# Segment attention written as four streams instead of a join after every unit

## The chip, the cores and the metric

The kernel runs on one core of a Trainium2 chip. The time is the device time of one execution in microseconds (us); the kernel before has a median of 3170.16 us over three runs (3165.81 to 3174.22). PE is TensorE, ACT is ScalarE, DVE is VectorE, POOL is GpSimd, and SP is SyncE, which here only issues DMAs.

## What is computed

Four layers follow each other, each with a layer norm ahead of it and a residual: A, B, A, B. Layer A is attention over the whole prompt with 32 query heads of width 16 that share one key and value head. Layer B cuts the 2048 rows into four segments of 512; each of its 32 heads attends within its segment (causal by segment) and also reads a memory that holds the key and value sums of the earlier segments.

```python
# A: prompt attention
scores = jnp.einsum("bhqd,bkd->bhqk", q, k) * (Dh ** -0.5)
o = jnp.einsum("bhqk,bkd->bhqd", softmax(scores), v)
...
# B: for each segment s
logits = jnp.einsum("bhqd,bhkd->bhqk", qs, ks) * scale + mask
a_dot = jnp.einsum("bhqk,bhkd->bhqd", softmax(logits), vs)
a_mem = einsum("bhld,bhde->bhle", phi(qs), M) / (einsum("bhld,bhd->bhl", phi(qs), z)[..., None] + 1e-6)
o = g * a_mem + (1.0 - g) * a_dot
M = M + jnp.einsum("bhld,bhle->bhde", phi(ks), vs)
z = z + phi(ks) summed over the segment
```

## The kernel before, in words

The host code writes the program as Python generators. Each generator yields a function that says from when PE may take its next piece, and the planner keeps rough clocks for PE, ACT, DVE and POOL (`clk`, `pe()`, `on()`) to choose which generator goes on. The order in which pieces are taken is nearly the order of the program on each engine; a scheduler behind it may still move single instructions forward or back.

Layer A works in units of four heads by 512 queries. For each of 16 key tiles of 128 keys a unit has scores on PE (L99/L102, operands qa and kst), two exps of 128 by 1024 on ACT (L752, into one of nine buffers named pa), and the product with the values (pa and va). These 1024 key tiles in all are the backbone. Beside them runs, for one segment at a time, `side`: the output projection of layer A and the norm, `b_block` (layer B's segment attention), the output projection of layer B, and the preparation of the next layer A. `weave` mixes the two in a given proportion. The last segment's `side` has no layer A work left beside it, so it runs alone at the end of the kernel.

`b_block` has eight units: pair t = n // 2 holds eight heads, and p = n % 2 picks four of them. These are the parts that the change touches, with the lines of the profile:

- inputs (`b_inputs`, one per pair): query and key projection (L455), their split into two fp16 parts (L551, L553), the way through DRAM (L893), the memory features ph (L907 to L909).
- row maxima (`rowmax`, from `b_load`, L933): the unit's scores once more on PE, a reduction per tile on DVE (L992; in the last block the masked form, L963, twelve reductions a unit, m), then the guard: a transposition on PE (L688), four small steps on DVE (L691 to L694), the maxima to DRAM (L696, mf) and back into two rows of the keys' and queries' tile (L698, qkb). `gr[n]` is the planner's time for that.
- scores (first half of `b_attend`): PE on qkb with 50 rows, so that the maximum is subtracted by the matmul, masks by idb and maskv, then six exps on ACT per unit (L1031). They take their space from the same nine pa buffers and the same two score banks as layer A (four banks, in two pairs).
- values and finish (second half of `b_attend`): PE on pa and vb, the transposition out of the bank on DVE (L1042), for all segments but the first the memory product (phq, ms; transposition L1051), the reciprocals and products (L1055 to L1067; in the last block L1062 to L1067 on POOL), and after a pair's second unit L1069, which puts the pair into otb. Then `b_memory` for odd units.

What sets the order of these is one line of `b_block`, a join per unit:

```python
for n in range(8):
    yield from par(rowmax(n + 2), unit(n), inputs(n // 2 + 2) if n % 2 == 1 and n // 2 + 2 not in hold else None)
```

`par` runs its generators together and ends when all have ended. So the scores and values of unit n, the maxima of unit n + 2, and for odd n the inputs of a later pair start together, and unit n + 1 starts when the last of them is through. Among the generators that are ready, `par` takes one whose matmuls have the form (the tiling of the PE array: rows, cols or full) that PE is in, else the first that is ready, else the one that is ready soonest. Ahead of the eight units stand the inputs of pairs 0 and 1 (in the last block of pair 2 too), the maxima of units 0 and 1, and the rest of the values' projection.

Of the kernel before, what the change touches and what calls it, by code (L numbers as in the profile page):

```python
# [89 lines left out]
def net_kernel(ctx, tc, x_in, a_wq, a_wk, a_wv, a_wo, b_wq, b_wk, b_wv, b_wo, b_beta, cst, out):  # L90
# [73 lines left out]
    LOAD = 2600.0  # L164
    LAG = 0.03
    DRAIN = 130.0
    FIRST = 3500.0
    PVL = 0.0
    PEND = 0.0
# [2 lines left out]
    tiling = ["full"]  # L172
# [211 lines left out]
    def form_of(need):  # L384
        return need.form() if isinstance(need, Need) else "full"

    def par(*gens):


        live = []  # L390
        for g in gens:
            if g is not None:
                try:
                    live.append([g, next(g)])
                except StopIteration:
                    pass

        def pick():
            ready = [z for z in live if z[1]() <= clk["pe"]]
            same = [z for z in ready if form_of(z[1]) == tiling[0]]  # L400
            return (same or ready or [min(live, key=lambda z: z[1]())])[0]

        while live:
            yield Need(lambda: min(z[1]() for z in live), lambda: form_of(pick()[1]))
            z = pick()
            try:
                z[1] = next(z[0])
            except StopIteration:
                live = [y for y in live if y is not z]
# [590 lines left out]

    b_ob = {}

    def b_attend(b, n, r, last):
        t, p = divmod(n, 2)
        exact = r["exact"]
        q, k = (qx, kx) if exact else (qb[n % 3], kb[n % 3])
        parts, held, tl = [], [], 0.0
        for kt in range(4):
            nq = 512 - kt * P
            es, loc = [], ([(0, 0), (1, 0)] if kt < 2 else [(0, 0), (0, nq)])  # L1010
            for s_ in range(1 if kt >= 2 else 2):
                yield Need(lambda: max(gr[n], rings["sc"].ready(), exps.ready()), "cols" if exact else "rows")
                ring = rings["sc"]
                z, sc = ring.take()
                for u in range(2):
                    if loc[u][0] != s_:
                        continue
                    o_ = loc[u][1]
                    if exact:
                        for i in range(2):  # L1020
                            by_triangle(i == 0, sc[:, i, o_:o_ + nq], k[0:98, 2 * u + i, kt * P:(kt + 1) * P],
                                        q[0:98, 2 * u + i, kt * P:512])
                        e_ = pe(2 * cols(nq) + 30, "cols")
                    else:
                        by_pairs(sc[:, :, o_:o_ + nq], k[:, u, kt * P:(kt + 1) * P], q[:, u, kt * P:512], 50, (0, 1),
                                 (maskv, 0))
                        e_ = pe(cols(nq) + 60, "rows")
                w = loc[1][1] + nq
                e = tmp(EXPS, [P, 2, 512], F32, "pa")
                held.append(exps.take()[0])  # L1030
                A.activation(e[:, :, 0:w], sc[:, :, 0:w], AF.Exp, scale=0.25 if exact else 0.25 / (UPB * UPB))  # L1031
                es.append(e)
                ring.free[z] = on("act", e_ + PEND, 51 + 1.667 * w)
                tl = ring.free[z] + HOP
            parts.append((kt, nq, es, loc))
        pvb, rel = yield from slot(None, max(tl, v_r[0]), "cols")
        for part in parts:
            b_pv(t, p, pvb, *part)
# [61 lines left out]
    def b_block(b, last, exact, norms):  # L1100

        hold = {}
        mem_done[:] = [-1] * 4

        def inputs(t):
            if t < 4:
                hold[t] = yield from b_inputs(b, t, exact, norms)

        def rowmax(*units):
            for n in units:  # L1110
                if n < 8:
                    need = b_load(hold[n // 2], n)
                    yield from b_rowmax(n, need, True) if exact else (b_rowmax_masked if last else b_rowmax)(n, need)

        def begin():
            yield from inputs(0)
            yield from rowmax(0, 1)

        def beside():
            yield from b_values((2, 3))  # L1120
            yield lambda: 0.0 if 0 in hold else 1e18
            yield from inputs(1)
            if last:
                yield from inputs(2)

        def unit(n):
            t = n // 2
            yield from b_attend(b, n, hold[t], last)
            if n % 2 == 1:
                yield from b_memory(b, t, hold[t])  # L1130

        if exact:
            yield from b_values((2, 3))
            for n in range(8):
                if n % 2 == 0:
                    yield from inputs(n // 2)
                yield from rowmax(n)
                yield from unit(n)
            return
        yield from par(begin(), beside())  # L1140
        if last:
            layout("b")
        for n in range(8):
            yield from par(rowmax(n + 2), unit(n), inputs(n // 2 + 2) if n % 2 == 1 and n // 2 + 2 not in hold else None)


    def everything(exact):
# [135 lines left out]
```

## Time and profile before

| | us |
|---|---|
| median of three runs | 3170.16 |
| the profiled execution | 3165.43 |
| its span, first to last instruction | 3163.6 |
| PE busy | 2796.1 |
| ACT busy | 2328.7 |
| DVE busy | 1554.7 |
| POOL busy | 269.4 |
| mean granted clock of PE | 0.976 |

The page shows one execution. Busy time is the union of an engine's instructions; a busy PE is not PE at its peak. The 40 slices of the page are 79 us each; a digit is the busy share or the granted clock in tenths. In a group's line the columns are line, engine, operation, output and inputs, count, busy time and mean ns, and the idle time of the engine ahead of the group with what ended it. In the chain each piece is start, duration, and what the end of the kernel waited for. Layer A's exps (L752) run from about 48 to about 2966 us; what comes after is the last segment's `side` alone. The exps of the eight blocks (L1031) begin at 481, 854, 1236, 1617, 2053, 2365, 2729 and 3036 us.

### The profile page before, as it was taken

Reading aid. Unit: us, or ns where it says so; the run is one execution under the profiler, and the core shown is the slowest. Engines: PE = TensorE matmul, PEld = TensorE weight load, DVE = VectorE, ACT = ScalarE, POOL = GpSimd, SP = SyncE. Lnnn points to the kernel's source line nnn. Section 1 sums busy time; section 2 is a strip of 40 time slices with the busy share of each in tenths; the row PEclk is TensorE's granted clock in tenths of the full one; section 3 lists DMA queues with packets and bytes.
Section 4 is the critical chain, followed back from the end, with each engine's and each line's share of the span. In section 5 each row is a group of like instructions: output and inputs, shape, how many; then the busy total and the mean of one; then the engine's idle time right before and its main releaser. Section 6 shows DMA issues by size and latency. Waiting matters only on the chain.

```text
span 3163.6 us, 115692 instructions
## 1 busy us (share of the span) xinstructions
PE 2796.1 (88%) x51714; PEld 1324.4 (42%) x51714; DVE 1554.7 (49%) x4463; ACT 2328.7 (74%) x2583; POOL 269.4 (9%) x437
## 2 busy tenths in 40 slices
PE   6988888899898998889998898888998899988987
PEld 3533344435443454334443344443443434433543
DVE  7621345534555435654365445464345533644455
ACT  4689778886778867887788878677687877878423
POOL 2100120001000010001100010000000000000111
PEclk9999999999999999999999999999999999999968
DMA  5320231113320233102331142320331114110331
GB/s 158 105 66 23 74 119 47 42 60 107 101 60 21 67 106 103 54 16 91 127 92 53 35 143 86 115 76 22 113 100 39 42 37 139 55 53 23 130 100 37
DMA packets 152444, 240.20 MB, mean 76 GB/s; under 512 B 26144, under 2 KB 101760, under 8 KB 151936
## 3 DMA queue, kind: packets, MB, share of 16 engines
q1 hardware_dynamic: 123520, 129.93, 13.6%
q0 software_dynamic: 28416, 102.77, 10.0%
q8 instruction: 407, 6.67, 0.9%
q14 instruction: 101, 0.83, 0.1%
HBM read 162.12 MB, written 70.52 MB: 74 GB/s over the span
## 4 chain that ended last, share of the span: by engine, by line
PE 38%; ACT 29%; issue 18%; DVE 8%; DMA 4%; POOL 1%; SPq 1%; DVEq 0%; ACTq 0%; POOLq 0%
ACT pa L752 25%; PE bank L99 17%; PE bank L455 13%; PE bank L102 7%; DVE mo L992 4%; ACT pa L1031 3%; DMA sb<-parts 2%; DVE m L963 1%; DMA xt<-in_A_x_dram 1%; DVE parts L553 1%; PE bank L515 0%; POOL parts L551 0%; DMA wst<-in_B_wq_dram 0%; DMA w<-wd 0%; PE bank L688 0%
## 5 line engine op out<-in xcount | busy, mean ns | idle before, releaser
L752 ACT ACTIVATE pa<-bank 128x1024 f32<-128x1024 f32 x2048 | 1947.2, 1107 | 469.6 <-PE bank L102 464.9
L102 PE MATMUL bank<-pa,va 64*17 64x512 f32 x14336 | 1101.7, 599 | 0.2 <-DVE t L791 0.2
L99 PE MATMUL bank<-pa,va 64*17 64x512 f32 x2048 | 1060.0, 598 | 10.3 <-ACT pa L752 5.8
L99 PE MATMUL bank<-qa,kst 49*32 49x512 f16 x2048 | 742.1, 382 | 179.0 <-ACT pa L752 146.9
L102 PE MATMUL bank<-qa,kst 49*32 49x512 f16 x14336 | 823.6, 387 | 0.8 <-DVE qmx L600 0.8
L992 DVE CUSTOM_DVE_ANT_0 mo<-bank,maskq 128x256 bf16<-128x256 f32 (+3 forms) x896 | 439.0, 490 | 223.3 <-PE bank L102 159.6
L99 PE MATMUL bank<-qkb 48*32 48x512 f16 (+7 forms) x1536 | 345.6, 311 | 111.1 <-DVE m L992 46.2
L102 PEld LDWEIGHTS <-kst 49*32 49x32 f16 x14336 | 227.6, 90 | 500.6 <-issue 489.5
L1031 ACT ACTIVATE pa<-bank 128x1024 f32<-128x1024 f32 (+2 forms) x384 | 323.3, 885 | 136.0 <-PE bank L102 133.1
L102 PE MATMUL bank<-qkb 50*32 50x512 f16 (+7 forms) x6656 | 367.8, 313 | 0.2 <-DMA qkb<-mf 0.2
L99 PEld LDWEIGHTS <-kst 49*32 49x32 f16 x2048 | 173.1, 92 | 371.2 <-issue 343.7
L455 PE MATMUL bank<-xh,w 128*128 128x512 f32 x832 | 285.6, 407 | 9.6 <-DVE w L319 4.8
L102 PEld LDWEIGHTS bank<-pa,va 64*17 64x17 f32 x14336 | 256.7, 94 | 24.7 <-DVE t L791 8.1
L455 PE MATMUL bank<-w,xh 128*128 128x512 f32 x752 | 247.5, 409 | 5.6 <-issue 4.1
L102 PEld LDWEIGHTS <-qkb 48*32 48x32 f16 (+1 forms) x6656 | 152.1, 94 | 222.8 <-issue 212.4
L99 PEld LDWEIGHTS bank<-pa,va 64*17 64x17 f32 x2048 | 185.5, 94 | 105.1 <-issue 15.5
L790 DVE STREAM_TRANSPOSE ts<-bank 128x512 f32<-128x512 f32 x88 | 62.9, 715 | 287.2 <-PE bank L102 286.9
L276 POOL DMA_DIRECT2D w<-wd x154 | 85.5, 556 | 1235.9 <-PE bank L455 1173.3
L455 PEld LDWEIGHTS bank<-xh,w 128*128 128x128 f32 x832 | 157.2, 189 | 79.8 <-issue 28.9
L99 PEld LDWEIGHTS <-qkb 48*32 48x32 f16 (+1 forms) x1536 | 129.2, 95 | 145.9 <-issue 109.6
L1042 DVE STREAM_TRANSPOSE t<-bank 128x512 f32<-128x512 f32 x64 | 45.9, 717 | 278.1 <-PE bank L102 278.1
L102 PE MATMUL bank<-pa,vb 128*17 128x384 f32 (+3 forms) x1920 | 173.5, 443 | 8.4 <-ACT pa L1031 7.6
(164 smaller groups left out, 2773.8 us busy)
## 6 DMA issues: line engine op xcount, KB each, us to landing
w<-wd POOLq DMA_DIRECT2D x154, 512.0 KB, 4.9
sb<-parts SPq DMA_DIRECT2D x192, 128.0 KB
qkb<-sb SPq DMA_DIRECT2D x256, 96.0 KB
wd<-w POOLq DMA_DIRECT2D x24, 512.0 KB, 3.9
x<-xt SPq DMA_DIRECT2D x48, 256.0 KB
xt<-x SPq DMA_DIRECT2D x48, 256.0 KB
qa<-sd SPq DMA_DIRECT2D x176, 66.0 KB
xt<-in_A_x_dram SPq DMA_DIRECT2D x32, 256.0 KB
```

What stands on the lines that cost most here:

```text
L99: nc.tensor.matmul(*a, **k)
L102: tc.keep_in_program_order(nc.tensor.matmul(*a, **k))
L276: G.dma_start(f(w), parts_d[kind, i])
L455: T.matmul(ps, lhsT=l_(kt), rhs=r_(kt), start=n == 0, stop=n == 11)
L553: V.scalar_tensor_tensor(parts[:, 1, :], x, up, parts[:, 0, :], op0=ALU.mult, op1=ALU.subtract)
L752: A.activation(x, sc, AF.Exp, scale=scale)
L790: V.transpose(ts.rearrange("p a b -> p (a b)"), pva[:, 0, :])
L963: V.reduce_max(m[:, u0:u0 + per, i, qt], ps[:, 0:per * nk].rearrange("p (h k) -> p h k", k=nk), axis=AX.X)
L992: V.tensor_tensor_reduce(out=mo[:, 0:nk], in0=ps[:, o_:o_ + nk], in1=maskq[:, 512 - nk:512], op0=ALU.add, op1=ALU.max, scale=1.0, scalar=- ...
L1031: A.activation(e[:, :, 0:w], sc[:, :, 0:w], AF.Exp, scale=0.25 if exact else 0.25 / (UPB * UPB))
L1042: V.transpose(t1.rearrange("p a b -> p (a b)"), pvb)
```

## The change

`b_attend` is cut in two: `b_scores` puts what it made into `scored[n]`, and `b_attend` takes it from there. The loop with its join goes. In its place `par` runs four generators from the first unit to the last, each with a condition of its own:

- `scores`: unit n when its maxima are written (`gr`) and n is at most one ahead of the finished units (AHEAD_S)
- `values`: unit n (values, finish, and the memory of odd units) when its scores are written
- `maxima`: unit n when the scores of unit n - 3 are written, n is at most two ahead of the finished units (AHEAD_M), and its inputs are there
- `pairs`: the inputs of pairs 2 and 3, when units 0 and 2 are finished

`par` gets an argument: with `same=False`, which the last block uses, it no longer prefers the form that PE is in, and takes the first ready generator in the order scores, values, maxima, pairs.

```diff
-    def par(*gens):
+    def par(*gens, same=True):
...
-            same = [z for z in ready if form_of(z[1]) == tiling[0]]
-            return (same or ready or [min(live, key=lambda z: z[1]())])[0]
+            alike = [z for z in ready if same and form_of(z[1]) == tiling[0]]
+            return (alike or ready or [min(live, key=lambda z: z[1]())])[0]
...
-    def b_attend(b, n, r, last):
-        t, p = divmod(n, 2)
+    def b_scores(n, r):
...
+        scored[n] = parts, held, tl
+
+    scored = {}
+
+    def b_attend(b, n, r, last):
+        t, p = divmod(n, 2)
+        parts, held, tl = scored.pop(n)
         pvb, rel = yield from slot(None, max(tl, v_r[0]), "cols")
...
-        for n in range(8):
-            yield from par(rowmax(n + 2), unit(n), inputs(n // 2 + 2) if n % 2 == 1 and n // 2 + 2 not in hold else None)
+        done = [0, 0]
+
+        def maxima():
+            for n in range(2, 8):
+                yield lambda: 0.0 if n <= done[0] + 2 and n <= done[1] + AHEAD_M and n // 2 in hold else 1e18
+                yield from rowmax(n)
+
+        def scores():
+            for n in range(8):
+                yield lambda: 0.0 if n in gr and n <= done[1] + AHEAD_S else 1e18
+                yield from b_scores(n, hold[n // 2])
+                done[0] = n + 1
+
+        def values():
+            for n in range(8):
+                yield lambda: 0.0 if n in scored else 1e18
+                yield from unit(n)
+                done[1] = n + 1
+
+        def pairs():
+            for t in range(2, 4):
+                yield lambda: 0.0 if done[1] >= 2 * t - 3 else 1e18
+                if t not in hold:
+                    yield from inputs(t)
+
+        yield from par(scores(), values(), maxima(), pairs(), same=not last)
```

The changed kernel has the same instructions on every engine, in another order; lines behind b_attend's second half are 8 higher, those between `par` and it 1 or 2 higher. Three places show what moves.

On DVE, in the last block, the end of unit 2's row maxima (m_52703, twelve reductions in all) and unit 0's finish (t_5248_53010). Before:

```order
L963 TENSOR_REDUCE m_52703<-bank 128x1
L692 SCALAR_TENSOR_TENSOR mrr_52690<-bank,mrr_52690 16x128
L693 TENSOR_REDUCE mmx_117<-bank 16x1
L694 TENSOR_TENSOR mmx_117<-mmx_117 16x1
L963 TENSOR_REDUCE m_52703<-bank 128x1 x5
L963 TENSOR_REDUCE m_52703<-bank 128x2 x4
L1042 STREAM_TRANSPOSE t_5248_53010<-bank 128x512
L691 TENSOR_SCALAR mrr_52985<-bank 16x128
```

After (unit 0's finish is t_5246_52905 to rr_52907; unit 1's begins with t_5260_53190):

```order
L965 TENSOR_REDUCE m_52703<-bank 128x1 x2
L1050 STREAM_TRANSPOSE t_5246_52905<-bank 128x512
L1053 COPY rr_52907<-t_5246_52905 128x16
L1059 STREAM_TRANSPOSE t_5248_52913<-bank 128x512
L1060 TENSOR_SCALAR rr_52907<-t_5248_52913 128x16
L1063 RECIPROCAL rr_52907<-rr_52907 128x32
L1065 TENSOR_SCALAR rr_52907<-rr_52907,g_46_183 128x16
L1072 TENSOR_SCALAR rr_52907<-rr_52907,gv_174 128x16
L965 TENSOR_REDUCE m_52703<-bank 128x1 x3
L965 TENSOR_REDUCE m_52703<-bank 128x2 x4
L1050 STREAM_TRANSPOSE t_5260_53190<-bank 128x512
L693 TENSOR_SCALAR mrr_53160<-bank 16x128
```

Unit 0's finish has moved ahead of seven of unit 2's reductions, and the guard of unit 2 (L691 before, L693 now) has moved from behind unit 0's values to behind unit 1's.

On DVE, at the end of the last block, the last row maxima (unit 7's, m_54403 before and m_54457 after) and its guard. Before, with unit 5's finish beginning in the third row; the finishes of units 6 and 7 follow further on:

```order
L963 TENSOR_REDUCE m_54403<-bank 128x1 x8
L963 TENSOR_REDUCE m_54403<-bank 128x2 x4
L1042 STREAM_TRANSPOSE t_5325_54710<-bank 128x512
L691 TENSOR_SCALAR mrr_54685<-bank 16x128
L1045 COPY rr_54712<-t_5325_54710 128x16
L692 SCALAR_TENSOR_TENSOR mrr_54685<-bank,mrr_54685 16x128
L693 TENSOR_REDUCE mmx_117<-bank 16x1
```

After; unit 6's first transposition, L1050, stands eight rows ahead of this piece, and the last row is unit 7's:

```order
L1065 TENSOR_SCALAR rr_54800<-rr_54800,g_46_183 128x16
L1072 TENSOR_SCALAR rr_54800<-rr_54800,gv_174 128x16
L965 TENSOR_REDUCE m_54457<-bank 128x2 x2
L1059 STREAM_TRANSPOSE t_5348_55068<-bank 128x512
L693 TENSOR_SCALAR mrr_54895<-bank 16x128
L1060 TENSOR_SCALAR rr_55062<-t_5348_55068 128x16
L694 SCALAR_TENSOR_TENSOR mrr_54895<-bank,mrr_54895 16x128
L695 TENSOR_REDUCE mmx_117<-bank 16x1
L696 TENSOR_TENSOR mmx_117<-mmx_117 16x1
L1278 TENSOR_SCALAR mmx_117<-mmx_117 16x1
L1279 TENSOR_TENSOR flag_119<-flag_119,mmx_117 16x1
L1050 STREAM_TRANSPOSE t_5346_55060<-bank 128x512
```

The last reductions and the guard of unit 7 have moved from ahead of unit 5's finish to behind unit 6's values. On PE 27 of the 48 matmuls of the last output projection now stand between that guard and the scores of unit 7.

On ACT, in the second woven block, the exps of layer A (L752 before, L754 after) and of the block's first two units (L1031 before, L1032 after). Before:

```order
L1031 ACTIVATE pa_13588<-bank 128x1024
L1031 ACTIVATE pa_13614<-bank 128x1024
L1031 ACTIVATE pa_13632<-bank 128x2x384
L1031 ACTIVATE pa_13650<-bank 128x2x384
L1031 ACTIVATE pa_13684<-bank 128x1024
L752 ACTIVATE pa_13700<-bank 128x1024
L752 ACTIVATE pa_13716<-bank 128x1024
L752 ACTIVATE pa_13738<-bank 128x1024
L752 ACTIVATE pa_13768<-bank 128x1024
L752 ACTIVATE pa_13790<-bank 128x1024
L1031 ACTIVATE pa_13844<-bank 128x2x256
L752 ACTIVATE pa_13866<-bank 128x1024
```

After:

```order
L1032 ACTIVATE pa_13588<-bank 128x1024
L1032 ACTIVATE pa_13614<-bank 128x1024
L1032 ACTIVATE pa_13632<-bank 128x2x384
L1032 ACTIVATE pa_13650<-bank 128x2x384
L1032 ACTIVATE pa_13684<-bank 128x1024
L1032 ACTIVATE pa_13724<-bank 128x2x256
L754 ACTIVATE pa_13740<-bank 128x1024
L754 ACTIVATE pa_13756<-bank 128x1024
L1032 ACTIVATE pa_13800<-bank 128x1024
L754 ACTIVATE pa_13810<-bank 128x1024
L754 ACTIVATE pa_13876<-bank 128x1024
L754 ACTIVATE pa_13886<-bank 128x1024
```

The sixth exp of unit 0 has moved ahead of five of layer A's, and the first exp of unit 1 (pa_13800) now comes three rows behind it.

More of the change, by code (lines that the diff above doesn't have):

```diff
@@ L166, in net_kernel @@
     DRAIN = 130.0
+    AHEAD_S = 1
+    AHEAD_M = 2
     FIRST = 3500.0
@@ L1102, in b_block @@
         hold = {}
+        gr.clear()
         mem_done[:] = [-1] * 4
@@ L1127, in unit @@
             t = n // 2
+            if exact:
+                yield from b_scores(n, hold[t])
             yield from b_attend(b, n, hold[t], last)
```

## Prediction

> **What bounds the kernel now.** I read the page first, then busy time by windows, then the PE waits of one window, then the chain and the timelines of the last block.
>
> ```profile
> span 3163.6 us, 115692 instructions
> ...
> PE 2796.1 (88%) x51714; PEld 1324.4 (42%) x51714; DVE 1554.7 (49%) x4463; ACT 2328.7 (74%) x2583; POOL 269.4 (9%) x437
> ...
> PEclk9999999999999999999999999999999999999968
> ```
>
> No engine is full over the span; PE is nearest, and its clock falls only at the end. The change touches b_block, which runs eight times: seven times woven with the prompt attention (scores and exps of L752), once alone at the end. I cut those eight stretches out, from each block's first row maxima to its last values.
>
> ```profile
> 437.00:665.00 228.00, 196.36 (x4385) 89.87 (x4370) 121.54 (x405) 180.56 (x200) 13.84 (x22) 0.97 0.17 49
> 817.00:1050.00 233.00, 204.77 (x4506) 90.09 (x4507) 133.15 (x437) 187.66 (x208) 9.66 (x15) 0.99 0.15 43
> 1199.00:1433.00 234.00, 206.09 (x4459) 90.37 (x4466) 132.78 (x433) 185.17 (x206) 9.69 (x15) 0.98 0.15 43
> 1577.00:1808.00 231.00, 206.24 (x4476) 89.34 (x4467) 126.15 (x413) 189.34 (x211) 10.52 (x17) 1.00 0.21 65
> 2011.00:2208.00 197.00, 166.51 (x3787) 77.47 (x3794) 119.62 (x403) 145.41 (x162) 9.39 (x15) 0.98 0.20 58
> 2327.00:2580.00 253.00, 223.55 (x4881) 95.90 (x4868) 131.81 (x432) 207.74 (x229) 9.84 (x15) 0.99 0.13 38
> 2684.00:2947.00 263.00, 230.76 (x4897) 99.84 (x4897) 136.62 (x442) 210.62 (x233) 10.19 (x16) 0.98 0.14 42
> 3026.00:3146.00 120.00, 103.96 (x2305) 50.59 (x2304) 80.69 (x198) 41.72 (x51) 17.01 (x26) 0.75 0.13 38
> ```
>
> The columns are the stretch, its length, busy PE, PEld, DVE, ACT and POOL, the granted clock, DMA share and GB/s. In the seven woven blocks PE idles 31.6 + 28.2 + 27.9 + 24.8 + 30.5 + 29.5 + 32.2 = 204.7 us: that is all that a better order could win there. In the last block (row eight) ACT is busy a third of the time, the clock is 0.75, and DVE and PE take turns. For the second window PE's own waits are:
>
> ```profile
> PE bank L99 <- ACT pa L752: 9.8, 28, 1.0
> PE bank L99 <- DVE m L992: 5.9, 11, 1.5
> PE bank L99 <- ACT pa L1031: 5.6, 17, 0.6
> ```
>
> These are many short waits (17 of them make 5.6 us; the longest for maxima is 1.5): no hole of several microseconds at the end of each unit. At the old join the planner gives PE the prompt's matmuls, so in the woven blocks the join was no wait but a choice of other work.
>
> **The last block, before.** Nothing lies beside it, so its chain is the end of the kernel.
>
> ```profile
> L1042 DVE STREAM_TRANSPOSE t<-bank x8: 708/718/718, 3052.3 to 3141.9; 128x512 f32<-128x512 f32 x8
> ```
>
> L1042 reads a unit's values; its eight starts are the beat. One beat, from unit 1 to unit 2, on DVE:
>
> ```profile
> 3066.37 0.72 DVE L1042 STREAM_TRANSPOSE t<-bank 128x512 f32<-128x512 f32 x1 [3.26 <-PE bank L102]
> ...
> 3069.29 0.69 DVE L963 TENSOR_REDUCE m<-bank 128x1 f32<-128x512 f32 x1
> 3071.37 0.71 DVE L1069 STREAM_TRANSPOSE otb<-obb 128x512 f32<-128x512 f32 x1 [1.39 <-POOL obb L1067]
> 3072.01 5.57 DVE L963 TENSOR_REDUCE m<-bank 128x1 f32<-128x512 f32 x11
> 3080.43 0.72 DVE L1042 STREAM_TRANSPOSE t<-bank 128x512 f32<-128x512 f32 x1 [2.86 <-PE bank L102]
> ...
> 3133.99 0.71 DVE L1042 STREAM_TRANSPOSE t<-bank 128x512 f32<-128x512 f32 x1
> ```
>
> The beat is 14.1 us: 2.9 of finish (to 3069.29), twelve maxima at about 0.5 to 0.6 each (6.3), 0.7 for L1069 after 1.4 of waiting, and 2.9 in which DVE waits for the next unit's values. The values stand behind all twelve maxima in PE's queue, and take a score bank only when a reduction frees one.
>
> ```profile
> 3038.95 3.55 ACT L1031 ACTIVATE pa<-bank 128x1024 f32<-128x1024 f32 x4 [21.77 <-PE bank L102]
> 3042.76 1.57 ACT L1031 ACTIVATE pa<-bank 128x1024 f32<-128x1024 f32 x2 [0.26 <-PE bank L102]
> ```
>
> ```profile
> 3041.44 3.17 DMA mf<-mrr
> 3044.63 0.60 SPq L698
> 3045.28 2.03 DMA qkb<-mf
> ...
> 3048.08 0.97 PE bank L99
> 3049.07 0.84 PE bank L99
> 3049.90 2.31 PE bank L102 x27
> 3052.21 0.21 PE bank L688
> ...
> 3146.82 7.54 PE bank L455 x31
> ```
>
> ```profile
> 854.14 0.30 SPq L696 DMA_DIRECT2D mf<-mrr  x1
> 855.47 1.31 SPq L698 DMA_DIRECT2D qkb<-mf  x2
> ```
>
> So a unit's six exps take 5.4 us (3038.95 to 3044.33), its values 4.1 in the half-clock stretch (3048.08 to 3052.21) and a projection matmul 7.54 / 31 = 0.24. The guard (a unit's maxima, sent through DRAM into the rows that its scores subtract) is 5.9 on its way in the last block (3041.44 to 3047.31). In a woven block it is 2.64 to the end of the second issue and with the same 2.03 of landing 4.7.
>
> **The change part by part.** Every engine has the same instructions as before; only their order differs, so each term is a wait.
>
> *Units 0 and 1 of the last block.* Unit 0's values now stand behind five of unit 2's maxima, not twelve. Its exps end at 3044.33, and with 4.1 for the values L1042 starts near 3048.3 instead of 3052.29: -4. Unit 1's scores follow on unit 0's values and memory matmuls (1.7 at this clock, an estimate from the 4.1 of the values, which have some 2.5 times the columns); its maxima have landed at 3047.31. With 0.6 to the first exp, 5.4 of exps, and 2 for the values' rest behind the last exp: 3048.3 + 1.7 + 0.6 + 5.4 + 2 = 3058.0 against 3066.37, so -8.4 in all so far.
>
> *Units 2 to 6.* Before: 3133.99 - 3066.37 = 67.6. Now a unit's maxima end one unit ahead, not two: the guard of unit n+1 follows unit n's values, and unit n+1's scores stand behind some eight of unit n+2's maxima. A beat is then 2.9 (finish) + 5 maxima (2.9, until the eighth has a bank) + 0.6 + 5.4 (exps) + 1.6 (values behind the last exp) = 13.4. The guard's trip of 4.7 to 5.9 is just hidden by the first 5.8. For the pair with the query projection I add 12 x 0.24 = 2.9; for the unit that has all twelve of the next maxima ahead of its scores, four more and two late ones, 6 x 0.55 = 3.3 and 1.8 of L826 and L827 work that falls on two beats; unit 4 has its maxima early and saves 1.4, unit 6 about 3.9. Sum: 13.4 x 5 + 2.9 + 3.3 + 1.8 - 1.4 - 3.9 = 69.7, so +2.1. Bounds: with DVE never waiting a beat is 9.9, five are 49.5, -18; with the guard's trip 2 us beyond its cover in each beat, +12. I stay by the sum, as PE, ACT and DVE hand over to each other in either order.
>
> *Unit 7.* Before it took 3141.9 - 3134.0 = 7.9, its maxima long landed. Now five of its maxima and its guard come behind unit 6's values: finish and reductions 2.9 + 5 x 0.55 + 0.9 = 6.5; then 27 of the 48 projection matmuls stand ahead of its scores, 27 x 0.24 = 6.6, which hide the guard's 5.9; then 0.7 + 5.4 + 0.6. That is 19.8: +11.9, and up to +18.5 if the 27 run at half clock.
>
> *Projection at the end.* Of the 31 matmuls behind the last transposition about 12 stay (three for each of four tiles): -19 x 0.24 = -4.6.
>
> Tail: -8.4 + 2.1 + 11.9 - 4.6 = +1.0.
>
> *Changes of tiling (same=not last).* The last block goes from 27 to 37 changes of matmul form. The guard's transposition, one such change and back, is 0.21 in the chain above; ten more are at most 2.1, and I take +1. [...]
>
> *The seven woven blocks.* Their order changes little: the same 55 to 89 prompt key tiles lie beside each block, and changes of form go from 489 to 480. What is new is that unit 1's first score tile follows its guard by one or two key tiles in four blocks, where it was four to fourteen. A key tile lasts 233 / 76 = 3.1 us, so 3.1 to 6.2 stand against the guard's 4.7 to 5.9: 0 to 2 us of PE wait in four blocks, I take +2 in all. The rest I put at 0, with a tenth of the 204.7 either way, +-20, as the bound: the waits above are short, and the prompt's matmuls fill what the join left.
>
> Sum: 1.0 + 1 + 2 = +4 on the span of 3163.6, so 3167.6, and 3169.4 for this execution (3165.4 before). That execution lies 0.15% under the median of 3170.16; on the median the forecast is **3174**, +0.13%: no change that a measurement of this kernel can tell, which takes about 0.3%, 9.5 us.
>
> **Rivals.** *The woven blocks gain.* With four streams the planner always has something of the side ready, and PE's waits for the block's own exps and maxima (5.9 + 5.6 of 26.6 us in the second window) shrink. At a tenth of 204.7 it is -20, so 3154. For it: these waits are there in all seven. Against it: the exps' order on ACT is nearly the same. Chance 0.20.
>
> *The clock rises in the last block.* The row above has 0.75 there. If PE's work closes up, the values (4.1 at half clock, 2.9 and less later) lose about 1.3 each and the maxima's matmuls follow: eight units, some -10, so 3164. For it: in the last stretch before the end the clock is back. Against it: PE still waits for exps once per unit. [...] Chance 0.07.
>
> *The lost lead shows (slower).* In the last block maxima come one unit ahead instead of two. If finish and maxima take less than the guard's trip and its issue, each of five beats waits some 2 us: +12 instead of +2, and unit 7 at the half clock +18.5 instead of +12. Then the tail is +18 and the sum +21, so 3191. It decides from the point where the trip passes 5.8 us; the chain shows 5.9. For it: that row, and nothing else covers unit 7. Against it: other trips were 4.7. Chance 0.28.
>
> *The change doesn't do what it says.* The scheduler sorts the instructions again by priority, and the woven order hardly moved; then only the last block differs. That is within my forecast, 3170.
>
> **How the numbers follow.** The forecast, 3174, has 0.45 (with the change that does nothing), the gain 0.20, the clock 0.07, the lost lead 0.28. Faster by over 0.3%: the gain, and 0.02 of the clock, which mostly ends within it: 0.22. Slower: the lost lead, and 0.05 of the forecast, where the woven +-20 lands high: 0.33. Within: 0.45 - 0.05 + 0.05 = 0.45. The range runs from the gain's 3154 to the lost lead's 3191, with some 2 or 3 beyond each, as each can come out larger: 3152 to 3194.
>
> **What would show it.** Right: L1042's line (L1050 now) starts at about 3048 for unit 0 and 3058 for unit 1, about ten earlier than before relative to the block's first maxima; unit 7 stands about 20 behind unit 6, with 27 projection matmuls in between; windows over the woven blocks keep their 28 us of idle PE each. Wrong: idle PE in the woven blocks under 24 or over 33 each; PE waiting for DMA qkb<-mf in every beat of the last block; a clock near 1.0 there.

## The result, and the profile after

| | before | after |
|---|---|---|
| median, same chip | 3168.64 us (7 runs) | 3182.78 us (7 runs) |
| ratio | | 1.0044, 95% interval 1.0032 to 1.0057 |
| profiled execution | 3165.43 | 3185.24 |
| its span | 3163.6 | 3183.4 |

The change makes the kernel slower by 0.44%, about 14 us. The page of the changed kernel:

```profile
span 3183.4 us, 115694 instructions
...
PE 2807.7 (88%) x51714; PEld 1329.3 (42%) x51714; DVE 1546.4 (49%) x4463; ACT 2323.8 (73%) x2583; POOL 268.4 (8%) x437
...
PEclk9999999999999999999999999999999999999978
```

PE has the same 51714 matmuls but is busy 11.6 us longer (2796.1 before), and idles 8.2 us more. The first question is where. I cut both traces where the program is at the same point: at the end of the prompt's 320th exp, which lies just ahead of the first block, and at the end of its last exp. Between the cuts lie the seven woven blocks and all that stands between them, and behind them comes the last segment alone. Busy time by windows, after (columns as in the prediction):

```profile
443.00:2983.00 2540.00, 2274.76 (x43414) 1057.48 (x43413) 1255.98 (x3797) 1950.29 (x2154) 172.25 (x280) 0.98 0.23 71
2983.00:3183.40 200.40, 163.86 (x2668) 95.29 (x2668) 114.98 (x280) 50.94 (x69) 29.29 (x49) 0.84 0.31 101
```

and before:

```profile
440.00:2966.00 2526.00, 2267.66 (x43422) 1054.23 (x43429) 1263.81 (x3797) 1954.35 (x2153) 172.81 (x280) 0.99 0.23 71
2966.00:3163.60 197.60, 162.98 (x2668) 95.40 (x2652) 115.77 (x280) 51.53 (x68) 29.59 (x48) 0.81 0.32 103
```

The woven part takes 2540 instead of 2526 us, +14: idle PE goes from 258.3 to 265.2 and busy PE from 2267.7 to 2274.8, at a granted clock of 0.98 for 0.99. The rest goes from 197.6 to 200.4, +2.8. So most of the loss lies in the woven part, where I had put +2. The 3 us that are left (443 for 440) lie ahead of the first cut; in the profiles of all kernels below this cut comes between 437.7 and 443.2 us, so they are scatter. PE's waits in the woven part, after:

```profile
PE bank L99 <- ACT pa L754: 113.7, 328, 1.0
...
PE bank L99 <- ACT pa L1032: 34.1, 94, 0.6
...
PE bank L102 <- ACT pa L1032: 10.7, 22, 0.8
```

and before:

```profile
PE bank L99 <- ACT pa L752: 120.5, 340, 1.0
...
PE bank L99 <- ACT pa L1031: 25.1, 75, 0.9
...
PE bank L102 <- ACT pa L1031: 6.6, 13, 0.9
```

PE waits less for the prompt's exps (120.5 to 113.7) and more for the block's own (25.1 + 6.6 = 31.7 to 34.1 + 10.7 = 44.8). The bracket at the end of a timeline row is the engine's idle time before it and what ended that. One place can be seen with the eye. On ACT in the first block, after:

```profile
484.85 4.92 ACT L1032 ACTIVATE pa<-bank 128x1024 f32<-128x1024 f32 x6
489.94 1.94 ACT L1032 ACTIVATE pa<-bank 128x1024 f32<-128x1024 f32 x2 [0.17 <-PE bank L102]
499.37 1.94 ACT L754 ACTIVATE pa<-bank 128x1024 f32<-128x1024 f32 x2 [7.50 <-PE bank L102]
```

and before:

```profile
481.32 4.92 ACT L1031 ACTIVATE pa<-bank 128x1024 f32<-128x1024 f32 x6
486.34 1.94 ACT L752 ACTIVATE pa<-bank 128x1024 f32<-128x1024 f32 x2
489.31 1.94 ACT L752 ACTIVATE pa<-bank 128x1024 f32<-128x1024 f32 x2 [1.04 <-PE bank L102]
```

Now unit 1's first two exps follow unit 0's six, and then ACT stands for 7.5 us. Eight of the nine pa buffers are then the block's. PE meanwhile runs unit 2's maxima one by one, each behind the reduction that frees its bank, and only then unit 0's values, which give the buffers back:

```profile
491.30 0.32 PE L99 MATMUL bank<-qkb 48*32 48x384 f16 x1
...
494.23 0.48 PE L99 MATMUL bank<-qkb 48*32 48x384 f16 x1 [0.43 <-DVE m L994]
...
496.32 0.37 PE L99 MATMUL bank<-qkb 48*32 48x256 f16 x1 [0.43 <-DVE m L994]
...
497.36 1.04 PE L99 MATMUL bank<-pa,vb 128*17 128x512 f32 x1 [0.43 <-DVE m L994]
```

Four windows of 3.41 us around that place:

```profile
488.39:491.80 3.41, 2.40 (x92) 1.11 (x89) 1.81 (x5) 3.24 (x4) 0.00 (x0) 1.00 0.30 79
491.80:495.21 3.41, 2.29 (x32) 0.68 (x32) 2.87 (x14) 0.07 (x1) 0.00 (x0) 0.50 0.15 43
495.21:498.63 3.42, 2.50 (x24) 0.58 (x27) 2.60 (x14) 0.00 (x0) 0.00 (x0) 0.50 0.02 5
498.63:502.04 3.41, 3.41 (x29) 0.93 (x21) 0.14 (x1) 1.94 (x2) 0.00 (x0) 0.50 0.00 0
```

The granted clock halves for three of them (0.50 for 1.00); the matmul of 48x384 takes 0.48 us there (494.23) and 0.32 ahead of them (491.30).

The last block shows the terms of the tail. The end of the prompt's last exp is the zero, before

```profile
2964.65 1.02 ACT L752 ACTIVATE pa<-bank 128x1024 f32<-128x1024 f32 x1 [0.84 <-PE bank L102]
```

and after:

```profile
2982.24 1.02 ACT L754 ACTIVATE pa<-bank 128x1024 f32<-128x1024 f32 x1 [0.85 <-PE bank L102]
```

The zero comes 17.6 us later (2983.26 against 2965.67). Six of the last block's eight units on DVE (0 to 2 and 5 to 7), after:

```profile
3065.74 0.72 DVE L1050 STREAM_TRANSPOSE t<-bank 128x512 f32<-128x512 f32 x1 [3.65 <-PE bank L102]
3073.41 0.72 DVE L1050 STREAM_TRANSPOSE t<-bank 128x512 f32<-128x512 f32 x1 [1.84 <-PE bank L102]
3089.85 0.72 DVE L1050 STREAM_TRANSPOSE t<-bank 128x512 f32<-128x512 f32 x1 [3.59 <-PE bank L102]
...
3140.57 0.72 DVE L1050 STREAM_TRANSPOSE t<-bank 128x512 f32<-128x512 f32 x1 [3.72 <-PE bank L102]
3147.84 0.72 DVE L1050 STREAM_TRANSPOSE t<-bank 128x512 f32<-128x512 f32 x1
3168.16 0.72 DVE L1050 STREAM_TRANSPOSE t<-bank 128x512 f32<-128x512 f32 x1 [13.03 <-PE bank L1283]
```

From the zero to unit 0 it is 86.6 us before and 82.5 after, from unit 0 to unit 1 14.1 and 7.7, from unit 1 to unit 6 67.6 and 74.4, from unit 6 to unit 7 7.9 and 20.3, and from there to the end of the span 21.7 and 15.2, which hold the projection.

### The profile page after: what moved, and what is told of

Same layout as the page of the kernel before. It is cut to its first block, busy times and chain, and to the rows that moved or that the text cites. A ratio compares the mean times of both kernels' runs of the same rounds, so it can differ in the third digit from the quotient of the medians.

```text
span 3183.4 us, 115694 instructions
## 1 busy us (share of the span) xinstructions
PE 2807.7 (88%) x51714; PEld 1329.3 (42%) x51714; DVE 1546.4 (49%) x4463; ACT 2323.8 (73%) x2583; POOL 268.4 (8%) x437
## 4 chain that ended last, share of the span: by engine, by line
PE 36%; ACT 30%; issue 19%; DVE 9%; DMA 4%; POOL 2%; SPq 1%; DVEq 0%; POOLq 0%; ACTq 0%
ACT pa L754 25%; PE bank L99 16%; PE bank L457 12%; PE bank L102 7%; DVE mo L994 4%; ACT pa L1032 4%; DMA sb<-parts 2%; DVE m L965 1%; DMA xt<-in_A_x_dram 1%; DVE parts L555 1%; DMA w<-wd 1%; POOL parts L553 0%; PE bank L517 0%; POOL w L278 0%; PE bank L690 0%
## 5 line engine op out<-in xcount | busy, mean ns | idle before, releaser
L754 ACT ACTIVATE pa<-bank 128x1024 f32<-128x1024 f32 x2048 | 1944.3, 1112 | 477.1 <-PE bank L102 471.7
L99 PE MATMUL bank<-qkb 48*32 48x256 f16 (+7 forms) x1536 | 348.5, 309 | 110.4 <-DVE m L994 43.4
L1032 ACT ACTIVATE pa<-bank 128x1024 f32<-128x1024 f32 (+2 forms) x384 | 324.8, 887 | 137.1 <-PE bank L102 135.4
L102 PE MATMUL bank<-qkb 48*32 48x512 f16 (+7 forms) x6656 | 369.4, 311 | 0.0
L102 PE MATMUL bank<-pa,vb 128*17 128x384 f32 (+3 forms) x1920 | 176.8, 454 | 12.4 <-ACT pa L1032 11.9
L1050 DVE STREAM_TRANSPOSE t<-bank 128x512 f32<-128x512 f32 x64 | 45.8, 716 | 278.3 <-PE bank L102 265.3
```

The lines of the kernel that those rows point to most:

```text
L99: nc.tensor.matmul(*a, **k)
L102: tc.keep_in_program_order(nc.tensor.matmul(*a, **k))
L754: A.activation(x, sc, AF.Exp, scale=scale)
L1050: V.transpose(t1.rearrange("p a b -> p (a b)"), pvb)
```

## The experiments

Theory: the loss arises in the woven blocks, from the order in which block and prompt work alternate there. Rivals: it arises in the last block; or it is the scatter of executions. The first four runs part these.

**Streams in the woven blocks only, or in the last only.** In the one the condition of the old loop is `last`, in the other `not last`:

```diff
-            if exact:
+            if exact or last:
                 yield from b_scores(n, hold[t])
...
+        if last:
+            for n in range(8):
+                yield from par(rowmax(n + 2), unit(n), inputs(n // 2 + 2) if n % 2 == 1 and n // 2 + 2 not in hold else None)
+            return
```

> Four streams in the seven woven blocks, the old join with its preference for the form in the last block. Theory 'woven order': the changed kernel's loss of some 14 us against before arises in the woven blocks; this kernel has all of that and nothing of the last block, so 11 to 13 us over before, ratio 1.0037, with a mean granted clock near 0.973 as in the seven runs of the changed kernel (0.971 to 0.975). Theory 'last block': the loss is the tail, which the one profile hides; then this kernel is within 3 us of before, ratio 1.000 to 1.001, clock 0.976. Theory 'one bad draw': what was seen ahead of the last block is the scatter of executions; then within 5 us of before as well.

> The old join in the seven woven blocks, four streams without the preference for the form in the last block. Theory 'woven order': only the tail's +2 us is left (its stretch from the first maxima to the end was 149.6 us against 147.5 in the two profiles), ratio 1.0006, no difference that can be told. Theory 'last block': +14 us, ratio 1.0044. In the profile unit 7's L1050 should stand some 20 us behind unit 6's, and the woven part should be as long as before's (last exp of the prompt attention near 2966 us).

> The changed kernel once more, for a second profile and times on the same chip: 3183 us, ratio 1.0044. If half-clock stretches in the woven blocks are made by the order, this profile shows them at the same places as the first (at about 492, 2076 us, 10 us each) and the mean clock is again 0.971 to 0.975; if they are chance, they lie elsewhere.

> The kernel before once more, for a second profile: 3169 us, mean clock 0.976. If the place of the half-clock stretches belongs to the order, they lie where they lay in the first profile, and some 54 us of them between 444 and 2900 us against 88 us in the changed kernel.

Measured: woven_only 3177.99 us, ratio 1.0018 (1.0006 to 1.0031); last_only 3172.01, 1.0007 (0.9996 to 1.0018); after_again 3182.19, 1.0036 (1.0021 to 1.0051); before 3171.60; before_again 3167.52. The profiles say more than the times, since steps of the same order agree within a few us. Cut at the two points above, the woven part takes 2526.0, 2530.4 and 2525.6 us in the three with the join (before, before_again, last_only), and 2541.4, 2540.1 and 2534.3 in the three with streams (woven_only, the changed kernel, after_again): +11.3 on the means. The part behind it takes 197.9, 197.1 and 196.5 with the join in the last block (before, before_again, woven_only), and 198.9, 200.1 and 197.4 with streams (last_only, the changed kernel, after_again): +1.6. ACT's 7.5 us in the first block are there in each of the three with streams in the woven blocks, and in none of the three with the join; in woven_only:

```profile
496.89 1.94 ACT L754 ACTIVATE pa<-bank 128x1024 f32<-128x1024 f32 x2 [7.49 <-PE bank L102]
```

So the order makes a loss in the woven blocks, by the profiles most of it; scatter alone is no explanation, since woven_only's interval leaves out 1. The +1.6 behind them is not clear of scatter: in the nine kernels with the join in the last block that part runs from 195.4 to 199.9. By the times woven_only (+0.18%, where 0.37 was forecast) and last_only (+0.07%) come to less than the whole (+0.36 and +0.44%), within their intervals.

The single place in the first block is no measure of the whole. Cut into 27 stretches of 64 prompt exps, the woven part with streams is longer in 17 of them, by 34 us in all and 5.4 at most, and shorter in ten, by 23 us in all and 7.3 at most (means of three profiles each): the 11 us are what is left over. The half-clock stretch at 492 is there again in after_again (6.8 us from 491.0, where it was 10.2). Over the woven part half clock lasts 89 and 68 us in the two profiles of the changed kernel, and 55 and 58 in the two of before; so some of it goes with the order and some with the execution.

**Why the woven order costs.** Three theories were put to the test, each with one edit on woven_only: early scores fill the buffers (AHEAD_S = 0 takes them back), values stand behind maxima because these have PE's form (`same=False`), maxima come too late (first in the list).

```diff
-    AHEAD_S = 1
+    AHEAD_S = 0
```

> As woven_only (streams in the seven woven blocks, the old join in the last), but with AHEAD_S = 0: a unit's scores start only when the unit ahead is finished. Theory 'full buffers': in woven_only and the changed kernel unit 1's scores take pa buffers (nine in all) while unit 0 still holds six, the prompt attention gets none until unit 0's values have run, ACT stands (7.5 us at 489 us; gaps of over 3 us between 400 and 2950 us sum to 155 to 160 us against 128 to 141 with the join), and PE, with only maxima to do, falls to half clock. Then this kernel loses the gap at 489, its gaps sum to under 145, and the woven part is 8 to 12 us shorter than in woven_only: 3168 to 3172, ratio to before 0.999 to 1.001. Theory 'maxima ahead of values': what hurts is that the values stand behind all the next maxima, whatever is ahead of them; then the gap stays at 5 us or more and the time within 3 us of woven_only, ratio 1.0018. Theory 'chance': 1.0018 as well, with the gap in another place.

```diff
-        yield from par(scores(), values(), maxima(), pairs(), same=not last)
+        yield from par(scores(), values(), maxima(), pairs(), same=False)
```

> As woven_only, but without the preference for the form PE is in (same=False in the woven blocks too): unit 0's values now come as soon as its exps are through, ahead of unit 2's maxima, while unit 1's scores may still run ahead. Theory 'full buffers': the values free the buffers early, so the gap at 489 us goes, but unit 1's block exps still push the prompt's back; 3 to 8 us under woven_only, if the further changes of form cost nothing; ratio 0.999 to 1.001. Theory 'maxima ahead of values': the whole loss goes, ratio 1.000. A price of the changes of form would show as busy PE over that of woven_only at the same clock.

```diff
-        yield from par(scores(), values(), maxima(), pairs(), same=not last)
+        yield from par(maxima(), scores(), values(), pairs(), same=not last)
```

> As woven_only, but the row maxima stand first in the list of the four, ahead of scores and values. The early scores of unit 1 stay. Theory 'full buffers': nothing better, the gap of some 7 us at 489 stays, ratio 1.002 within 0.001. Theory 'late maxima': if the loss came from the maxima being served last, it goes: ratio 1.000.

Measured: woven_s0 3181.12, ratio 1.0051 (1.0031 to 1.0071); woven_anyform 3141.41, 0.9917 (0.9896 to 0.9939); woven_maxfirst 3206.39, 1.0122 (1.0100 to 1.0143). All three lie outside what was forecast for them. In woven_s0 the gap at 489 is gone, as expected, and the time is no better; ACT's gaps of over 3 us still sum to 151 us, where under 145 was expected. That speaks against the full buffers, though not alone, since AHEAD_S = 0 can cost something itself; woven_valfirst below settles it. The late maxima fall, with the wrong sign: in woven_maxfirst PE's waits for the maxima's reductions are 81.0 us in the woven part, where woven_only has 56.6. Without the preference for the form the same four streams are 0.8% faster than before, some 27 us, and 1.0% faster than with it, some 32 us. The woven part of woven_anyform, and PE's waits in it:

```profile
439.00:2936.00 2497.00, 2258.27 (x43408) 1053.47 (x43407) 1261.50 (x3797) 1954.36 (x2153) 172.96 (x280) 0.99 0.23 72
```

```profile
PE bank L99 <- ACT pa L754: 97.6, 283, 1.5
...
PE bank L99 <- ACT pa L1032: 34.0, 95, 0.8
```

PE idles 238.7 us there, 26.5 less than in the changed kernel, and 16.1 of that are waits for the prompt's exps (113.7 to 97.6) and 8.1 waits for the block's own (44.8 to 34.0 + 2.7). In the first block ACT goes on with the prompt's exps right behind unit 1's first two:

```profile
483.95 1.94 ACT L1032 ACTIVATE pa<-bank 128x1024 f32<-128x1024 f32 x2 [1.76 <-PE bank L102]
485.78 2.93 ACT L754 ACTIVATE pa<-bank 128x1024 f32<-128x1024 f32 x3
489.69 4.90 ACT L754 ACTIVATE pa<-bank 128x1024 f32<-128x1024 f32 x5 [0.99 <-PE bank L102]
```

**What in the preference costs, and do the streams matter?** If values that wait behind maxima were the cause, it would be enough to take values whenever they are ready, and the old join with the unit first would gain as well. And if early scores still did harm, AHEAD_S = 0 would add to the gain.

```diff
-            alike = [z for z in ready if same and form_of(z[1]) == tiling[0]]
+            alike = [z for z in ready if same and form_of(z[1]) == tiling[0]]
+            alike = [z for z in ready if first is not None and z[0] is first] or alike
...
+        vals = values()
-        yield from par(scores(), values(), maxima(), pairs(), same=not last)
+        yield from par(scores(), vals, maxima(), pairs(), same=not last, first=vals)
```

> As woven_only (last block with the old join), the preference for the form kept in the woven blocks, but values are taken whenever they are ready, whatever form PE is in. Theory 'late values': the loss of woven_only came of ready values standing behind the next unit's maxima, since these have PE's form; then this kernel has all or most of woven_anyform's gain: 3140 to 3150, ratio 0.991 to 0.994, and the gap of ACT at 489 us is gone. Rival 'any preference costs': the gain comes from the other pieces (inputs, maxima, scores) being taken in the list's order; then 3165 to 3178, ratio 0.999 to 1.002. Rival 'clock': refuted already if the clock time lost stays near 40 us at a gain.

The kernel before, with its `par` given the argument `same`:

```diff
+            more = inputs(n // 2 + 2) if n % 2 == 1 and n // 2 + 2 not in hold else None
-            yield from par(rowmax(n + 2), unit(n), ...)
+            if last:
+                yield from par(rowmax(n + 2), unit(n), more)
+            else:
+                yield from par(unit(n), rowmax(n + 2), more, same=False)
```

> The kernel before, its join kept in all blocks, but in the seven woven ones the unit (scores and values) stands first in the list and the maxima second, without preference for the form. Theory 'late values': what counts is that values come as soon as their exps are through, not the four streams: 3142 to 3152, ratio 0.991 to 0.994. Rival 'streams': without the next unit's scores beside it the join gains little: 3163 to 3172, ratio 0.998 to 1.001.

woven_anyform with AHEAD_S = 0:

> As woven_anyform, with AHEAD_S = 0: the next unit's scores wait until the unit is finished. If the early scores still hold buffers that the prompt attention needs, this is some 5 us faster, 3134 to 3138. If they do good (the exps of the next unit run while the values' finish is on its way), it is 5 to 15 us slower, 3146 to 3156. From woven_s0 against woven_only (3 us slower) I lean to the second, at the small end: 3146.

The changed kernel with `same=False` in every block:

> The changed kernel with one argument turned: no preference for the form in any block (same=False), so four streams everywhere. woven_anyform plus the last block of last_only: 3141 + 2 to 3 us (last_only was 2.2 over before, its end stretch 2.5 longer), 3144, ratio to before 0.9925. Rival: the two do not add, since the last block's planning starts from other clocks; then 3136 to 3150.

Measured: woven_valfirst 3175.69, ratio 1.0017 (1.0003 to 1.0031); join_unitfirst 3182.30, 1.0049 (1.0033 to 1.0064); woven_anyform_s0 3161.00, 0.9977 (0.9967 to 0.9988); all_anyform 3142.78, 0.9917 (0.9904 to 0.9931). My theory of late values falls with the first two. The full buffers fall with woven_valfirst too: there the early scores stay, ACT's gap at 489 us is gone (1.4 us are left), and the time is that of woven_only. The rival of the late values, that any preference costs, had 0.999 to 1.002 and is not refuted. The gain needs both: no preference for the form, and the next unit's scores beside the values of this one (AHEAD_S = 0 gives back 0.6 of the 0.8%). join_unitfirst lies outside both of its forecasts, and woven_anyform_s0 15 us above its own. all_anyform came within 1.3 us of its forecast; it and woven_anyform beat both kernels, before and after, by the same ratio.

PE's waits in the woven part show what each half of the pair does. In join_unitfirst:

```profile
PE bank L99 <- ACT pa L752: 99.4, 285, 1.9
...
PE bank L99 <- DMA qkb<-sb: 25.9, 15, 4.2
```

The waits for the prompt's exps are 97.2 to 100.3 us in all four kernels without the preference in the woven blocks, with streams or with the join, and 113.7 to 120.5 in the ten with it. So the preference costs some 17 us of these waits in the streams, with early scores (114.0 to 97.6) and without (117.1 to 100.3), and some 20 in the join, where the list's order changed as well. Without the early scores what is won there goes elsewhere, at least in part: the waits for the inputs' way through DRAM (qkb<-sb) are 25.9 and 23.7 us in join_unitfirst and woven_anyform_s0, where woven_anyform has 16.2, and the clock lost (last table) is 44.4 and 41.0 us for 29.0.

**The last block with the maxima first.** On last_only:

```diff
-        yield from par(scores(), values(), maxima(), pairs(), same=not last)
+        yield from par(maxima(), scores(), values(), pairs(), same=not last)
```

> The old join in the woven blocks, in the last block the four streams without preference and with the maxima first in the list. Unit 7's maxima then lie two units ahead again. My term for unit 7 (+11.9 in the prediction, for maxima that come behind unit 6's values) should go, while units 0 and 1 keep part of their gain: the stretch from 15 us ahead of the block's first guard to the end, 141.4 us in last_only and 139 in before, falls to about 130 to 134; ratio to before 0.997 to 0.999. Rival: with the maxima ahead of the values again the beat of before comes back, 139 us, ratio 1.000.

Measured: 3172.94, ratio 1.0011 (0.9999 to 1.0023), no gain, as the rival had it. Four of its eight units on DVE, the first, the third, the sixth (3120.80) and the last, and the first of unit 7's reductions (L965):

```profile
3055.85 0.72 DVE L1050 STREAM_TRANSPOSE t<-bank 128x512 f32<-128x512 f32 x1 [2.99 <-PE bank L102]
...
3070.42 0.72 DVE L1050 STREAM_TRANSPOSE t<-bank 128x512 f32<-128x512 f32 x1 [0.36 <-PE bank L102]
...
3120.80 0.72 DVE L1050 STREAM_TRANSPOSE t<-bank 128x512 f32<-128x512 f32 x1 [2.88 <-PE bank L102]
...
3122.37 0.65 DVE L965 TENSOR_REDUCE m<-bank 128x1 f32<-128x512 f32 x1
...
3151.74 0.72 DVE L1050 STREAM_TRANSPOSE t<-bank 128x512 f32<-128x512 f32 x1 [10.28 <-PE bank L102]
```

From unit 0 to unit 2 it takes 14.6 us, where before took 28.1, and from unit 2 to unit 7 81.3, where before took 61.4. What the first units win the last ones give back: unit 7's maxima start behind unit 5's values (3122.37 against 3120.80), where in before they start 10.5 us ahead of them (3116.68 against 3127.17). AHEAD_M asks only that unit 4 is finished, so what holds them until then is not shown.

All profiles, cut at the same two points (us; "clock lost" is half the length of the half-clock records in the woven part):

| kernel | woven part | its PE busy | its PE idle | clock lost | rest, to the span's end | ratio timed |
|---|---|---|---|---|---|---|
| before | 2526.0 | 2267.4 | 258.6 | 27.3 | 197.9 | 1 |
| before_again | 2530.4 | 2269.8 | 260.6 | 29.0 | 197.1 | |
| last_only | 2525.6 | 2265.2 | 260.3 | 25.6 | 198.9 | 1.0007 |
| last_maxfirst | 2529.5 | 2267.0 | 262.5 | 25.6 | 198.4 | 1.0011 |
| after | 2540.1 | 2274.8 | 265.3 | 44.4 | 200.1 | 1.0044 |
| after_again | 2534.3 | 2267.2 | 267.1 | 34.1 | 197.4 | 1.0036 |
| woven_only | 2541.4 | 2273.2 | 268.2 | 42.7 | 196.5 | 1.0018 |
| woven_valfirst | 2537.8 | 2273.3 | 264.5 | 41.0 | 196.5 | 1.0017 |
| woven_s0 | 2541.3 | 2274.0 | 267.3 | 34.1 | 197.2 | 1.0051 |
| woven_maxfirst | 2564.3 | 2282.5 | 281.8 | 49.5 | 197.4 | 1.0122 |
| join_unitfirst | 2534.1 | 2272.5 | 261.6 | 44.4 | 199.9 | 1.0049 |
| woven_anyform_s0 | 2521.7 | 2268.9 | 252.8 | 41.0 | 195.4 | 0.9977 |
| woven_anyform | 2497.6 | 2258.4 | 239.2 | 29.0 | 196.0 | 0.9917 |
| all_anyform | 2494.4 | 2255.0 | 239.4 | 25.6 | 201.8 | 0.9917 |

Each row is one execution, and rows of one order lie up to 7 us apart. Eight orders of the same work make the woven part 2494 to 2564 us long. Idle PE spans 43 of these 70 us, busy PE 28. Half-clock time does not explain the order of the rows: woven_anyform_s0 loses 41.0 us and is still shorter than before. The clock's share of the changed kernel's 11 us stays open, as no run varied the clock alone. Open too is why the preference for the form makes PE wait for the prompt's exps: three guesses at a single cause fell, and what is shown is that the pair of choices decides, and in which waits.

## Why the prediction was right or wrong

The time of 3182.78 lies within the range, but on the side that I gave 0.33: slower by more than 0.3%. That the range holds it is in part luck: its upper end was built for a loss in the last block, and the loss came in the woven ones.

*Units 0 and 1.* Right. Unit 0 comes 4.1 us earlier (predicted 4), unit 1 then 10.5 earlier in all (predicted 8.4).

*Units 2 to 6.* Right in direction, too small: 74.4 for 67.6, +6.8 (predicted +2.1, bounds -18 to +12). One term that was mis-sized is "1.6 (values behind the last exp)". The end of the exps and of the values, for units 2, 3 and 4:

```profile
3081.01 5.11 ACT L1032 ACTIVATE pa<-bank 128x1024 f32<-128x1024 f32 x6 [9.21 <-PE bank L102]
3086.44 3.33 PE L102 MATMUL bank<-pa,vb 128*17 128x512 f32 x27
...
3100.64 1.59 ACT L1032 ACTIVATE pa<-bank 128x1024 f32<-128x1024 f32 x2 [0.26 <-PE bank L102]
3104.39 1.90 PE L102 MATMUL bank<-pa,vb 128*17 128x512 f32 x27
...
3115.22 0.60 ACT L1032 ACTIVATE pa<-bank 128x512 f32<-128x512 f32 x1 [0.92 <-PE bank L102]
3117.98 2.92 PE L102 MATMUL bank<-pa,vb 128*17 128x512 f32 x27
```

From the last exp to the last value it is 3.6, 4.1 and 5.1 us; 28 of unit 2's 32 values and all of units 3's and 4's start behind the last exp, those of units 2 and 4 in large part at half clock (the granted clock is 0.57 and 0.65 in these two stretches, and 1.00 in unit 3's). In the beats of units 5 and 6 it is 0.5 and 1.5. The five come to 14.8 where I had 5 x 1.6 = 8.0, so 6.8 too little; I missed by 4.7, so the other terms came out some 2 us too large together, which was not taken apart.

*Unit 7.* Right: 20.3 for 7.9, +12.4 (predicted +11.9). The 27 projection matmuls stand between the guard and unit 7's scores, as read from the order:

```profile
3153.03 0.71 PE L457 MATMUL bank<-w,xh 128*128 128x512 f32 x2
...
3159.21 0.40 PE L457 MATMUL bank<-w,xl 128*128 128x512 f32 x1
```

They take 6.6 us (3153.03 to 3159.61, predicted 6.6). In after_again and last_only unit 7 takes 18.6 us, as its values run in 2.35 us there, where this profile has 4.0 at a granted clock of 0.58.

*Projection at the end.* From unit 7 to the end of the span 21.7 falls to 15.2, -6.5 (predicted -4.6). The sum of the tail in this pair of traces is -10.5 + 6.8 + 12.4 - 6.5 = +2.2, on the means above +1.6, and by last_only's ratio +2.2, with 0 inside its interval; I had +2 with the changes of tiling. This part of the prediction held, and its sum better than its terms, whose errors (-2.1, +4.7, +0.5, -1.9) nearly cancel.

*Changes of tiling.* I took +1 in the last block, from 0.21 us in the chain; that is the chain's piece of the transposition itself (L688, 0.28 us by its records in before) and no price of a change. Between the two cuts the matmuls of woven_anyform change 808 times between the tile sizes of scores, values and projections, where those of the changed kernel do so 787 times, and PE is busy 2258.4 us there instead of 2274.8. No run here changes the number of changes alone, so the price of one is not shown, and the +1 neither; 21 more of them did not keep the order from being faster, and keeping the form in these streams costs some 32 us.

*The seven woven blocks.* This step failed: "The rest I put at 0". It measured +11 (2538.6 for 2527.3 on the means of three). I argued from counts that stayed the same (key tiles beside each block, changes of form) and from waits that are short. Both held. The first and the last of the seven block windows, after:

```profile
440.00:670.00 230.00, 198.43 (x4334) 88.12 (x4318) 118.95 (x400) 176.44 (x196) 14.29 (x23) 0.94 0.17 49
...
2703.00:2965.00 262.00, 231.51 (x4969) 100.15 (x4949) 136.85 (x442) 212.58 (x237) 10.16 (x16) 0.99 0.15 46
```

PE idles 31.6 and 30.5 us in them, 205.0 in all seven, against 204.7 before: by the sign that I named, nothing had changed. It was too weak a sign, since the windows leave out the stretches between the blocks. Over the whole woven part idle PE is 7.0 us more and busy PE 4.3, on the means of three. Of the waits, those for the block's own exps grow by 13 (31.9 to 44.9), and those for the prompt's exps and for the maxima shrink by 12.6 together; many small ones make up the rest. For the busy PE the half clock is a candidate (the granted clock of the first block is 0.94 where it was 0.97), but no run shows its share. The 11 us lie within the +-20 that I had named as the bound; as a forecast the term was wrong. What I did price there, 2 us of guard trips in four blocks, is not in the trace: PE's waits in the woven part hold no DMA qkb<-mf at all.

*The rivals.* "The woven blocks gain" did not happen in this kernel. With `same=False` there is a gain of some 27 us, more than the 20 that I gave as the bound, but not by the waits that I named: those for the block's own exps are above before's (36.7 for 31.7), and those for the prompt's exps shrink. "The lost lead shows" is right only on the outside, slower: its place, waits on the guard's trip in the last block, is empty: PE's matmuls wait for DMA qkb<-mf nowhere in the last block, and for unit 7 the 27 projection matmuls hide it (the second issue of the trip, L700, ends at 3157.01, the matmuls at 3159.61). "The clock rises in the last block" did a little (0.81 to 0.84 in the last windows above) without a gain in time; that it rises as PE's work closes up was my estimate, and no run shows it.

## What to carry to other kernels

Where a planner interleaves two streams that hand over between PE and ACT, equal counts and short waits do not make two orders equal: the same work took 2494 to 2564 us here, and no count made beforehand told which order was the better. Split such a change by stage and by argument before judging it; here one flag (`same=False`) turned 0.4% slower into 0.8% faster. A gain at the front of a chain of units (unit 1 came 10.5 us earlier) is worth little if the last unit's maxima still wait for the one before, as they did here.

## What the runs showed of the hardware

In the woven parts of before and after the granted clock falls to a half for stretches of 3.4, 6.8 or 10.2 us (13 of them in before, 16 in after), and all its changes lie on one grid of 3.41 us. One stretch began at 491.80 behind a window in which PE was busy 2.40 of 3.41 us (70%), with no wait over 0.5 us; what set it off is not shown. The busy share alone does not decide: on this grid half clock began behind windows of 0 to 76% busy PE in these two profiles, and others with 53 to 62% kept the full clock.

Two executions of one program differ here in few places. Cut into 27 stretches of 64 prompt exps, the two profiles of before agree within 0.25 us in 16 and within 1.1 in 24; the two of the changed kernel in 14 and in 19, and there the largest difference is 5.4. Single profiles, cut at the same instruction, so show a change of a few us where the times of whole executions scatter by 10 and more (3162.49 to 3177.23 in 26 runs of before).
